# A fused mLSTM and mixture-of-experts kernel: the first phase cut into finer steps and put in a new order

## The chip, the cores and the metric

One core of a Trainium2 chip runs the whole program. Its engines are TensorE (PE, with its weight loads as PEld), VectorE (DVE), ScalarE (ACT), GpSimd (POOL) and SyncE (SP), which issues most of the DMAs. The metric is the device time of one execution in microseconds (us). The kernel before has a median of 782.83 us over three runs (781.64 to 783.22).

## What is computed

Three stages follow each other: a gated linear attention (mLSTM) over 4 batches of 768 tokens with 8 heads of 40, a dense feed-forward layer with a per-channel leaky slope, and a top-1 mixture of 8 experts with a softmax gate and a sigmoid output gate.

```python
def _attn_ref(q, k, v, i_gate, f_gate, o_gate):
    ...
    for t in range(S):
        m_new = np.maximum(f_gate[:, :, t] + m, i_gate[:, :, t])
        f_stab = np.exp(f_gate[:, :, t] + m - m_new)
        i_stab = np.exp(i_gate[:, :, t] - m_new)
        m = m_new
        C = f_stab[:, :, None, None] * C + i_stab[:, :, None, None] * np.einsum('bhd,bhe->bhde', vt, kt)
        n = f_stab[:, :, None] * n + i_stab[:, :, None] * kt
        ...
        denom = np.maximum(np.abs(nq), 1.0)
        y[:, :, t] = o * h_tilde / denom

def _moe_ref(x, w_in, w_out, alpha):        # x is 3072 x 320, w_in 320 x 2048
    h = x @ w_in
    g = np.maximum(h, 0.0) + alpha * np.minimum(h, 0.0)
    return (g @ w_out).astype(np.float32)

def _moe2_ref(x, w_gate, w_output_gate, w1, w2):
    e_idx = np.argmax(x @ w_gate, axis=1)
    ...
    out[mask] = gate_w[mask, None] * eom[mask, e, None] * (np.maximum(x[mask] @ w1[e], 0.0) @ w2[e])
```

## The kernel before

**Two phases.** The first phase does attention, the dense layer and the preparation of the expert weights; the second runs the experts on slots of 128 sorted tokens. Only the first phase's head is touched here.

**Attention units.** The tokens are 24 units of 128 (`u`; batch `u // 6`, chunk `u % 6`). For each unit `load_g` brings the cumulated gates back from DRAM in two halves (tile `D`), `att_e` takes their exponential on ACT and masks it on POOL, `att_s` (L704) makes the products of queries and keys (`ps`) and multiplies them by `D` on DVE (L713), `att_h` and `att_d` read and update the running state, `att_b` multiplies by the values (`pa`), `att_y` normalises on DVE in four steps, and `att_c` transposes the result into `xT`. A unit's state comes from the unit ahead of it.

**Gates.** `gates`, `gates_e` and `gates_d` turn the gate inputs into `G` (stored to DRAM as `gd`), `EKT` and `DEC`, in three parts that cover one, two and three chunks. They borrow the two buffers of `v` and the three of `xr`.

**Weights.** The dense weights arrive as 64-bit floats in three buffers `raw`. `dec_wi` and `dec_wo` turn each piece into 32-bit floats in three integer instructions on DVE (L614, L616, L618). `split_wi` and `split_wo` split them into a rounded high part (ACT) and a residual (POOL or DVE). `gate_w` and `gate_w2` append the products with the gate weights. The expert weights go through the same `raw` buffers: `expert_load`, `expert_split`, `expert_store`.

**Dense layer.** Three units make a block of 384 tokens, and each block has 16 chunks of 128 hidden channels; `k` counts the 128 chunks of all blocks. `ffn1` (code F, eight products into a bank `ph`, L834) is followed by a negated Relu on ACT (L842) and `ph <- v*(1-alpha)+ph` on DVE (L843). `ffn_split` (code g) makes the high part on ACT (L849) and the residual on DVE (L850), both read from `ph`. `ffn2` (code S) adds nine products into three banks `acc` (L862, L863, L865). There are two `ph` banks and two `v` buffers. The first F needs the first block's `xT`, that is the units 0, 1 and 2 in sequence. F0 and S12 below mean the first F and the thirteenth S.

**What sets the order.** `ORDER` is a written list of step codes, and every engine gets its instructions in the order of that list. Each engine works its own list strictly in order and waits on semaphores for the others. `OTHER` names the indices of a step that go to the other of DVE and POOL. POOL can't read PSUM. The step `warm` (L1172) is a product of zeros, 128x128 by 128x512, that nobody reads.

```python
            A.activation(v, ph[:, :384], AF.Relu, scale=-1.0)
            V.scalar_tensor_tensor(ph[:, :384], v, al1[:, i : i + 1], ph[:, :384], ALU.mult, ALU.add)
            gt[k] = ph[:, :384]
```

Of the kernel before, what the change touches and what calls it, by code (L numbers as in the profile page):

```python
# [8 lines left out]
F32 = mybir.dt.float32  # L9
# [8 lines left out]
P = 128  # L18
# [25 lines left out]
KR = 64 + D  # L44

OTHER = {
    "prep_kt": (
        1, 3, 4, 7, 8, 9, 13, 14, 15, 16,  # L50
    ),
    "att_y": (
        0, 1, 2, 4, 7, 11, 13, 16, 17, 18, 19, 20, 21, 22, 23,
    ),
    "expert_split": (
        0, 1, 2, 3, 5, 6, 7, 8, 10, 12, 13, 14, 15, 18, 19, 20, 25, 26, 27, 30, 31, 32, 33, 34, 35, 36,
        37, 38, 39, 40, 41, 42, 43, 44, 45, 46, 47, 48, 49, 50, 51, 52, 53, 54, 55, 56, 57, 58, 59, 60,
        61, 62, 63,
    ),
    "split_wi": (  # L60
        0, 1, 3, 5, 13, 14,
    ),
    "split_wo": (
        2, 4, 10, 15,
# [5 lines left out]
for _n, _w in (  # L70
# [11 lines left out]
lo load_gates do load_cst load_gates lo lo gates do gates_e lq gates gates_e do do warm ah so load_g ae gw do do so  # L82
do do gw load_wg load_sel li gates_d gates_d lv pt lv di di di si gv gv do lo do do do load_g ae as lg ad so so log
sg li li gw gw lq li di di di di load_g ab ay pt ay load_g di load_gates si ah ay ay di si ad ae di di di ac lo do
warm warm si load_g load_g do gv ae as ae lo lq do do do do warm ab ay so so ay ay gv ay gw warm lo lo lo warm warm
warm lg gw do ae do do do so as do lv ac gv lq lq ah gates ab set_al1 gv ay gw lo do do gw warm warm so li pt do
warm lg warm warm gates_e do so load_g ay ay ay warm do do gates_d gw di do di warm warm di lv ac warm warm warm ad
pt si el load_g es li di di lo gv gv F di load_g F g et ah si ae do g lo do do ae S F gw as so so load_g warm g S
gw do do li di log do so ae li di ad di lv gv gv F gw di di di ae F as lg load_g ah si lo si g do do ae g S S lg lg
li do so di ab ay ay ay pt di el es lq gw di li di log F F di di et g g ad si pt li di li di di si di di sg gv lo  # L90
lq sg si el S S load_g ay F F g S di ah do lv ab si do load_g do es li et F g gv li lv ay ac ay lo ay ay di g S S
ae ae di as so gw di di di F F ab di g g si li lv ac load_g di ay si S di load_g load_g li gv do di S ay el do ay
do ay F gv ae si F g di di S ae S pt lg lo g lq lq di as el ae si ad so ad pt F ac load_g do g do do ab ay ay S so
gw gw es ah log ay et ay F gv gv g lg es F g as S ah F F g ab et load_g S ae g load_g ae ay ay ay el ad bo el el es
es F F lg load_g ae S ac load_g lv ae S pt et g S g es ah lq lv ad F ay g F S as lq ah F et ab ay S g g ac el ay et
es lv el F F as S g es load_g ae lg lg et ay lq ay S sg S et g F ab ay load_g bp lg S g ac S pt el ad F F S g g S
el el es lq es F g F g ay ay ay ah pt S pt S et es F S et g F log ad g ae et as ae S bo F g F load_g ae ab ay el lv
el S g ay es el F as g load_g load_g es et es et F load_g ac lv ah el el ae ae lg lg S g S S F g ad pt ah ay es F g
ab F ay ad et ae et S g el load_g el F es ay et F ay ay ac S g es ae S g ah F S S et es ay et g lv el el bp as F F
el g es et pt S S ab ac g ad F F g S g ay lq sg es es S ay lv pt F ay el lq g F as S g F et es ah ad S log S g bo F  # L100
sg et g load_g load_g ay el el F lg S ae ab ay ay ay et S F S g lq lq S g ae ac lg el S as lv load_g load_g load_g
es et es et ay F pt F g g ab ae ay ac F S g es ay ay ay S F F ae as lq S g g load_g ah ad ac ae el F lv pt el ae g
et ab ay ay S es es F et et g load_g ay F S g as ay lv S load_g S F g F ah ab ay S el el es ad lg ay ae g ay el es
F ac g load_g et et ah ah lv es et ae bp ay S S S ae as F g F load_g bo g ab ae load_g ae F g S lq el S ac F g
load_g pt S pt F lg load_g ae as el es lq F S g S el g es et F et g ay ay el F ae ab g ay ay ay F load_g lv F S lq
S ad g g es et es et el ad pt ae ac S F g S el el as F F log g S S g es et lg bp es et F F g S g S load_g el S es
et F g F log el el ae ay ay g S S bo es F lg F ah g S es as sg ay et et g F g lq ab ay S F g el el S es load_g
load_g sg F F S g ay ad g es ae ac et S lv et ay ay pt F es F ah ab ay ay lg el ae g S g es ay lv ad pt S F F el g
ac ah et es et S load_g ay ae g el el F es S g lg S ad F et es F lq et et g el el ac bp S g S S F g F S es es g F g
et S S bo as el es F F g et lv pt el el et as ab ay es et ay ay load_g S S g lg el load_g first_set ah lq ab el ay  # L110
ay F g F S g ad ae es F F lv es g S g ac S S ae ay ay ay as et et es et ac F g F S el el el bp g F ah ab g es es ay
ay ay ay F F S S S g g et es et el S et el F g F el S es es g F et et ac g S S es et F g ld el el F g S F g S bo ld
es F F S g g route_a S F F S g el g S bh bh bh et ld ld ld ad bh ld ld bh bh bh F ld S ld es S ld ld g es F g bh bh
S bh bh F g F S et bh ld g ld S bp F F ld bh g bh bh bh bh S S bh route_first bh bh bh g F route_first2 first_rows
S g F g ld S F F S ld ld g S ld ld ld pt ld ld g first_x first_x S bo bp et first_1 route_b first_1 route_c first_t
first_s first_tl route_c2 first_t first_tl first_s first_2 first_2 route_d first_st first_2 first_2
# [19 lines left out]
    "di": ("dec_wi", [(i, j) for i in range(16) for j in range(3)]),  # L136
    "gates_e": ("gates_e", zip(range(3))),
# [12 lines left out]
    "warm": ("warm", zip(range(20))),  # L150
# [31 lines left out]
def mlstm_moe_kernel(  # L182
# [262 lines left out]
    with ExitStack() as p1:  # L445
# [70 lines left out]
        def gates(part):  # L516
            c0, c1, o = GPARTS[part]
            nn, n = c1 - c0, (c1 - c0) * P
            fs = slice(c0 * P, c1 * P)
# [3 lines left out]
            gx[part] = GG, w  # L523
# [5 lines left out]
            V.tensor_tensor(g[:, 1:], tf[:, 1:], m[:, : n - 1], ALU.add)  # L529
            lo = 1 if part == 0 else 0  # L530
            V.tensor_tensor(g[:, lo:], g[:, lo:], m[:, lo:], ALU.subtract)
            V.tensor_copy(mlast, m[:, n - 1 : n])
# [3 lines left out]
            V.tensor_tensor(w, ti, m, ALU.subtract)  # L536
            V.tensor_tensor(w, w, GG, ALU.subtract)
            nc.sync.dma_start(gd[:, fs], GG[: B * H])

        def gates_e(part):  # L540
            c0, c1, o = GPARTS[part]
            nn, n = c1 - c0, (c1 - c0) * P
            GG, w = gx[part]
            V.tensor_tensor(
# [105 lines left out]
        def gate_w(i):  # L650
# [3 lines left out]
            for k in range(3):  # L654
                c0 = min(k * P, DM - P)
                T.transpose(pt[:, k * P : (k + 1) * P], f[:, c0 : c0 + P], ident)
# [666 lines left out]
```

## Time and profile before

| | kernel before |
|---|---|
| median of three runs | 782.83 us |
| the profiled execution: its time, its span | 782.92 us, 781.1 us |
| TensorE matmul busy, weight loads busy | 751.7 us (96%), 714.8 us (92%) |
| VectorE busy | 472.0 us (60%) |
| ScalarE busy | 363.2 us (47%) |
| GpSimd busy | 164.9 us (21%) |
| granted TensorE clock, mean | 0.990 |

The shares are means over a program whose head and body differ. A reader first looks at the busy time of each engine stretch by stretch, then at where TensorE stands idle or runs slowly, and then at what the engine that it waits for does in that stretch. A matmul's end is modelled, so the start times tell more than the busy share.

### The profile page before, as it was taken

What the parts mean: (1) busy time and instruction counts of PE and PEld (TensorE: products, weight loads), DVE (VectorE), ACT (ScalarE), POOL (GpSimd) and SP (SyncE); (2) the same over time, 40 slices, a digit from 0 to 9 for tenths busy, and PEclk for the clock granted to TensorE, in tenths of its full rate; (3) what the DMA queues carried; (4) which work ended last, traced back from release to release, by engine and by line L of the source; (5) the groups of instructions that cost most, each with busy time, mean ns of one, the idle gap of its engine ahead of it and who ended that gap; (6) DMA issues with size and microseconds to landing.
All of it is one profiled execution on the core that took longest, in us unless ns stands there. A gap on an engine that the chain in (4) does not pass through costs nothing. (4 is left out here: it accounts for less than half of the span.)

```text
span 781.1 us, 15245 instructions
## 1 busy us (share of the span) xinstructions
PE 751.7 (96%) x4931; PEld 714.8 (92%) x4931; DVE 472.0 (60%) x1159; ACT 363.2 (47%) x810; POOL 164.9 (21%) x225
## 2 busy tenths in 40 slices
PE   2899999999999999999999999999999999999995
PEld 2787999989999999999999999998999999999994
DVE  4878998775767566767687786867332232232231
ACT  3536666636664654655565354433333233233231
POOL 1222433203130323210000000012232232232232
PEclk9988999999999999999999999999999999999998
DMA  6938877876788785766977868795977645921000
GB/s 194 258 111 262 271 243 231 258 234 242 230 283 296 236 294 179 234 234 245 307 255 257 294 240 303 274 340 189 383 305 292 240 171 201 428 83 39 29 22 13
DMA packets 81787, 179.64 MB, mean 230 GB/s; under 512 B 8700, under 2 KB 39481, under 8 KB 80428
## 3 DMA queue, kind: packets, MB, share of 16 engines
q1 hardware_dynamic: 78252, 169.92, 63.4%
q0 software_dynamic: 3456, 8.71, 3.3%
q8 instruction: 45, 0.74, 0.4%
q14 instruction: 34, 0.28, 0.1%
HBM read 246.55 MB, written 55.59 MB: 387 GB/s over the span
## 5 line engine op out<-in xcount | busy, mean ns | idle before, releaser
L834 PE MATMUL ph<-ring 128*128 128x384 f32 x1024 | 196.7, 340 | 0.0
L834 PEld LDWEIGHTS ph<-ring 128*128 128x128 f32 x1024 | 177.0, 188 | 1.8 <-DVE ring L850 0.4
L862 PE MATMUL acc<-ring 128*128 128x336 f32 x384 | 123.4, 326 | 0.5 <-ACT ring L849 0.5
L863 PE MATMUL acc<-ring 128*128 128x336 f32 x384 | 119.6, 317 | 0.0
L842 ACT ACTIVATE v<-ph 128x384 f32<-128x384 f32 x128 | 62.3, 489 | 114.5 <-PE ph L834 114.2
L843 DVE SCALAR_TENSOR_TENSOR ph<-v,al,ph 128x384 f32<-128x384 f32 x128 | 78.3, 618 | 53.2 <-ACT v L842 52.8
L409 DVE TENSOR_SCALAR yo<-po,xg 128x320 f32<-128x320 f32 x26 | 14.3, 551 | 137.3 <-PE po L289 137.3
L289 PE MATMUL po<-ring,hh 128*128 (+1 forms) x432 | 95.6, 308 | 0.0
L289 PE MATMUL p<-ring,xh 128*128 (+1 forms) x324 | 89.9, 398 | 0.0
L850 DVE TENSOR_TENSOR ring<-ph,ring 128x384 fp32r<-128x384 f32 x128 | 70.3, 553 | 31.4 <-ACT ring L849 29.7
L849 ACT ACTIVATE ring<-ph 128x384 fp32r<-128x384 f32 x128 | 62.1, 488 | 52.9 <-DVE ph L843 43.4
L865 PE MATMUL acc<-ring 128*128 128x336 f32 x384 | 80.2, 317 | 0.0
L289 PEld LDWEIGHTS po<-ring,hh 128*128 128x128 f32 x432 | 73.2, 187 | 2.3 <-ACT hh L389 0.2
L862 PEld LDWEIGHTS acc<-ring 128*128 128x128 f32 x384 | 72.3, 188 | 1.9 <-ACT ring L849 0.9
L863 PEld LDWEIGHTS acc<-ring 128*128 128x128 f32 x384 | 72.3, 188 | 0.0
L389 ACT ACTIVATE hh<-p 128x512 fp32r<-128x512 f32 x54 | 29.4, 595 | 86.5 <-PE p L387 86.5
L289 PEld LDWEIGHTS p<-ring,xh 128*128 128x128 f32 x324 | 58.8, 188 | 11.3
L289 PE MATMUL po<-ring,hl 128*128 (+1 forms) x216 | 66.5, 308 | 0.2 <-DVE hl L391 0.2
L376 ACT ACTIVATE hr<-p 128x512 f32<-128x512 f32 x56 | 33.4, 597 | 67.3 <-PE p L289 63.7
L865 PEld LDWEIGHTS acc<-ring 128*128 128x128 f32 x384 | 63.5, 189 | 0.2 <-DVE ring L850 0.2
L700 ACT ACTIVATE D<-D,EKT 128x128 f32<-128x128 f32 x192 | 60.7, 393 | 3.5 <-DMA D<-gd 3.3
L410 POOL DMA_INDIRECT out_dram<-yo,tok x28 | 28.1, 1003 | 160.8 <-DVE yo L409 146.2
(197 smaller groups left out, 1139.6 us busy)
## 6 DMA issues: line engine op xcount, KB each, us to landing
ring<-scr SPq DMA_DIRECT2D x26, 3072.0 KB
ring<-scr SPq DMA_DIRECT2D x26, 2560.0 KB
ring<-scr SPq DMA_DIRECT2D x33, 512.0 KB
D<-gd SPq DMA_DIRECT2D x48, 256.0 KB
er<-in_ew_dram SPq DMA_DIRECT2D x32, 384.0 KB
scr<-ring SPq DMA_DIRECT2D x32, 384.0 KB
scr<-er SPq DMA_DIRECT2D x32, 384.0 KB
er<-in_ew_dram SPq DMA_DIRECT2D x32, 320.0 KB
```

The source lines that it names most:

```text
L289: mm = T.matmul(o_, lhsT, r, start=start, stop=stop)
L376: A.activation(hr_half(j, hf), ph, AF.Relu)
L389: A.activation(hh[:, hs], pts[j, hf], AF.Copy)
L700: A.activation(d[:, j], d[:, j], AF.Exp, bias=EKT[:, c, i + j : i + j + 1])
L834: T.matmul(ph[:, :384], wi_[i][lo][:, wc], xTs[n % 2][:, xc], start=(a == 0), stop=(a == len(PASSES) - 1),)
L842: A.activation(v, ph[:, :384], AF.Relu, scale=-1.0)
L843: V.scalar_tensor_tensor(ph[:, :384], v, al1[:, i : i + 1], ph[:, :384], ALU.mult, ALU.add)
L849: A.activation(gh, v, AF.Copy)
L850: V.tensor_tensor(gl, v, gh.bitcast(F32), ALU.subtract)
L862: T.matmul(ac, gh[:, sl], hi, start=(i == 0), stop=False)
L863: T.matmul(ac, gh[:, sl], lo, start=False, stop=False)
L865: T.matmul(accs[n][t][:, :NO], gl[:, t * P : (t + 1) * P], hi, start=False, stop=(i == NFC - 1))
```

## The change

1. The products and the step that reads their bank become separate steps: `att_s` is cut into `att_s` and `att_m`, `att_h` into `att_h` and `att_n`, `att_d`/`att_u`, `att_b`/`att_a`, `att_c`/`att_x`, `gate_w`/`gate_c`, `gate_w2`/`gate_s`, `ffn1`/`ffn_act`, and `gates` into `gates`, `gates_g`, `gates_w` and `gates_st`. The list can place the halves apart.
2. The first 450 entries of `ORDER` stand in another order. Up to the thirteenth S both lists hold the same steps; behind it they are the same entry by entry. 15 of the 20 products `warm` are gone.
3. For the first 24 chunks (`KEEP`) the leaky result stays in the SBUF buffer `v` and not in the bank `ph`.
4. `OTHER` moves work: the residuals of 14 of those 24 chunks go from DVE to POOL (9 of them among the first 14 chunks), the output-gate product of units 0, 1, 2, 4 goes to POOL and that of 3 and 5 to DVE, the residuals of the expert pieces 0 and 1 go to POOL, and some `split_wi`, `split_wo` and `prep_kt` change sides.

```diff
+KEEP = 24
 OTHER = {
+    "ffn_split": (
+        0, 1, 2, 6, 8, 9, 10, 12, 13, 14, 16, 18, 20, 22,
+    ),
     "att_y": (
-        0, 1, 2, 4, 7, 11, 13, 16, 17, 18, 19, 20, 21, 22, 23,
+        3, 5, 7, 11, 13, 16, 17, 18, 19, 20, 21, 22, 23,
     ),
...
 ORDER = """
-lo load_gates do load_cst load_gates lo lo gates do gates_e lq gates gates_e do do warm ah so load_g ae gw do do so
+lo do do do load_gates gates load_cst ah lo gw load_gates warm gates_g gates_w do do load_sel gates_e gc lo do
...
+        def gates_st(part):
+            c0, c1, o = GPARTS[part]
+            nc.sync.dma_start(gd[:, c0 * P : c1 * P], gx[part][0][: B * H])
...
+            t["pp"] = pp
+
+        def att_m(u):
+            t = ut[u]
+            pp = t["pp"]
             for hf in range(2):
                 d = t["D", hf].rearrange("p h t -> p (h t)")
                 V.tensor_tensor(d, pp[hf], d, ALU.mult)
...
+            gt[k] = ph
+
+        def ffn_act(k):
+            ph = gt[k]
+            i = k % NFC
             v = hp.tile([P, 384], F32, tag="v", bufs=2, name=f"v_{k}")
             A.activation(v, ph[:, :384], AF.Relu, scale=-1.0)
-            V.scalar_tensor_tensor(ph[:, :384], v, al1[:, i : i + 1], ph[:, :384], ALU.mult, ALU.add)
-            gt[k] = ph[:, :384]
+            g = v if k < KEEP else ph[:, :384]
+            V.scalar_tensor_tensor(g, v, al1[:, i : i + 1], ph[:, :384], ALU.mult, ALU.add)
+            gt[k] = g
 
         def ffn_split(k):
             v = gt[k]
             gh, gl = gsp[k % 3]
             A.activation(gh, v, AF.Copy)
-            V.tensor_tensor(gl, v, gh.bitcast(F32), ALU.subtract)
+            engine(V, G, "ffn_split", k).tensor_tensor(gl, v, gh.bitcast(F32), ALU.subtract)
```

ScalarE's list before, from the sigmoid of the first output gates (`so`) to the exponentials of unit 1 (`D_0_298`, `D_1_313`); `f_wi` and `f_wo` are weight pieces, `woT` a transposed piece, `pt` the transpose of unit 0:

```order
L499 ACTIVATE so_268<-so_268 128x960
L657 ACTIVATE woT_276<-pw_275 128x384
L657 ACTIVATE woT_282<-pw_281 128x384
L630 ACTIVATE ring<-f_wi_292 128x384
L630 ACTIVATE ring<-f_wi_296 128x384
L700 ACT_TABLE_LOAD
L700 ACTIVATE D_0_298<-D_0_298,EKT 128x128 x4
L821 ACTIVATE ring<-pt_351 128x3x128
L630 ACTIVATE ring<-f_wi_347 128x384
L666 ACTIVATE ring<-pwg_373 128x16
L700 ACTIVATE D_1_313<-D_1_313,EKT 128x128 x4
```

The same place now, where unit 1 has the tiles `D_0_316` and `D_1_330`:

```order
L523 ACTIVATE so_278<-so_278 128x960
L699 ACTIVATE woT_296<-pw_244 128x384
L668 ACTIVATE ring<-f_wi_275 128x384
L668 ACTIVATE ring<-f_wi_293 128x384
L746 ACT_TABLE_LOAD
L746 ACTIVATE D_0_316<-D_0_316,EKT 128x128 x4
L746 ACTIVATE D_1_330<-D_1_330,EKT 128x128 x4
L668 ACTIVATE ring<-f_wi_310 128x384
L900 ACTIVATE ring<-pt_364 128x3x128
```

Both halves of unit 1 now stand together, ahead of unit 0's transpose and of a third weight piece.

TensorE's list before, ahead of the first F, which follows the last row by some more `warm`, `pd` and `pwg`; `pe_ek` and `pe_dec` are the third part of the gates, `pt_640` the transpose of unit 2 (four more rows of `warm` are left out behind the first):

```order
L656 MATMUL pw_567<-cst,f_wo_478 128x128 x3
L1172 MATMUL warm_573<-ring 128x512
...
L554 MATMUL pe_ek_594<-cst,w_525 128x96 x3
L1172 MATMUL warm_610<-ring 128x512
L572 MATMUL pe_dec_616<-gin,sel 120x12 x3
L656 MATMUL pw_623<-cst,f_wo_565 128x128 x3
L1172 MATMUL warm_633<-ring 128x512
...
L819 MATMUL pt_640<-cst,y_606 128x128 x3
```

The same place now, down to the first F (`ph_631`):

```order
L592 MATMUL pe_ek_541<-cst,w_493 128x96 x3
L1257 MATMUL warm_548<-ring 128x512
L1257 MATMUL warm_558<-ring 128x512
L693 MATMUL pw_569<-cst,f_wo_468 128x128 x3
L1257 MATMUL warm_583<-ring 128x512
L693 MATMUL pw_597<-cst,f_wo_565 128x128 x3
L890 MATMUL pt_603<-cst,y_579 128x128 x3
L610 MATMUL pe_dec_608<-gin,sel 120x12 x3
L706 MATMUL pwg_620<-wgt,woT_573 128x16 x3
L808 MATMUL pd_625<-kv_2_517,kt 120x123 x3
L913 MATMUL ph_631<-ring 128x384 x8
```

The row of five products of zeros ahead of `pe_ek` is gone; three stand singly or in a pair behind and one ahead of it, and the transpose of unit 2 comes ahead of `pe_dec`.

GpSimd's list now, behind the mask of unit 3's first half; `v_676`, `v_679` and `v_739` are the results of the first three F, `er` an expert piece:

```order
L747 AFFINE_SELECT D_0_591<-D_0_591 128x512
L935 TENSOR_TENSOR ring<-v_676,ring 128x384
L935 TENSOR_TENSOR ring<-v_679,ring 128x384
L935 TENSOR_TENSOR ring<-v_739,ring 128x384
L747 AFFINE_SELECT D_1_593<-D_1_593 128x512
L1186 TENSOR_TENSOR er_735<-er_735,ring 128x768
L1186 TENSOR_TENSOR er_737<-er_737,ring 128x768
```

The three residuals and the two expert pieces stood on VectorE.

## Rows read from the trace of the kernel before

**Rows 1.** Stretches: from:to, length, busy PE, PEld, DVE, ACT, POOL; granted clock, DMA

```profile
55.00:60.00 5.00, 4.36 (x21) 3.96 (x21) 4.93 (x18) 0.67 (x2) 0.00 (x0) 0.50 0.24 72
...
0.00:128.00 128.00, 109.28 (x676) 100.32 (x676) 104.44 (x265) 69.30 (x174) 36.09 (x52) 0.96 0.75 227
...
86.00:127.00 41.00, 40.98 (x289) 39.95 (x288) 37.61 (x90) 27.24 (x65) 15.09 (x20) 1.00 0.80 252
...
150.00:160.00 10.00, 8.70 (x58) 8.39 (x58) 8.09 (x23) 7.18 (x19) 2.88 (x7) 1.00 0.88 265
160.00:700.00 540.00, 539.70 (x3599) 518.91 (x3599) 321.01 (x792) 252.66 (x546) 98.63 (x138) 1.00 0.74 261
```

**Rows 2.** Timeline of TensorE: start, duration, work, idle before it in brackets

```profile
53.43 3.57 PE L778 MATMUL pa<-kv,D 128*128 128x41 f32 x16
...
60.15 2.48 PE L1172 MATMUL warm<-ring 128*128 128x512 f32 x5
...
68.47 3.04 PE L834 MATMUL ph<-ring 128*128 128x384 f32 x16
...
89.32 1.87 PE L778 MATMUL pa<-kv,D 128*128 128x41 f32 x16
...
126.47 0.62 PE L865 MATMUL acc<-ring 128*128 128x336 f32 x3
```

**Rows 3.** Waits of VectorE, 0 to 71.5 us: total, times, longest

```profile
DVE f_wo L614 <- DMA r_wo<-in_wo_dram: 3.9, 1, 3.9
DVE DEC L580 <- PE pe_dec L572: 2.4, 2, 1.5
DVE G L535 <- DMA cst<-in_consts_dram: 1.9, 1, 1.9
DVE D L713 <- PE ps L710: 1.6, 2, 1.2
DVE pa L788 <- PE pa L778: 1.4, 1, 1.4
DVE dn L797 <- PE pa L778: 1.4, 1, 1.4
```

**Rows 4.** Groups of VectorE, 0 to 128 us: busy us, mean ns

```profile
L618 DVE SCALAR_TENSOR_TENSOR f_wi<-r_wi,f_wi 128x384 int32<-128x384 int32 x15 | 9.0, 597 | 0.2
...
L850 DVE TENSOR_TENSOR ring<-ph,ring 128x384 fp32r<-128x384 f32 x14 | 7.5, 547 | 0.0
...
L1101 DVE TENSOR_TENSOR er<-er,ring 128x768 fp32r<-128x768 f32 x3 | 2.9, 950 | 0.0
...
L807 DVE TENSOR_TENSOR y<-y,so 128x320 f32<-128x320 f32 x4 | 2.0, 491 | 0.1
```

**Rows 5.** Timeline of VectorE, columns as in Rows 2

```profile
24.16 1.29 DVE L713 TENSOR_TENSOR D<-ps,D 128x512 f32<-128x512 f32 x2
...
40.33 1.29 DVE L713 TENSOR_TENSOR D<-ps,D 128x512 f32<-128x512 f32 x2 [0.43 <-PE ps L710]
...
50.64 0.69 DVE L713 TENSOR_TENSOR D<-ps,D 128x512 f32<-128x512 f32 x1 [1.20 <-PE ps L710]
...
71.50 0.61 DVE L843 SCALAR_TENSOR_TENSOR ph<-v,al,ph 128x384 f32<-128x384 f32 x1
...
114.51 1.20 DVE L618 SCALAR_TENSOR_TENSOR f_wi<-r_wi,f_wi 128x384 int32<-128x384 int32 x1
```

**Rows 6.** Timeline of ScalarE at the exponentials of unit 1

```profile
34.22 0.53 ACT L630 ACTIVATE ring<-f_wi 128x384 fp32r<-128x384 f32 x1 [4.69 <-DVE f_wi L618]
...
36.05 1.28 ACT L700 ACTIVATE D<-D,EKT 128x128 f32<-128x128 f32 x4
```

**Rows 7.** Groups of GpSimd over the whole span: busy us, mean ns

```profile
L631 POOL TENSOR_TENSOR ring<-f_wi,ring 128x384 fp32r<-128x384 f32 x10 | 10.1, 1014 | 13.2 <-ACT ring L630 13.2
L1101 POOL TENSOR_TENSOR er<-er,ring 128x768 fp32r<-128x768 f32 x5 | 9.2, 1840 | 32.8 <-ACT ring L1100 13.7 <-DMA scr<-er 13.5 <-DMA qg<-in_qg_dram 5.5
```

**Rows 8.** Timeline of GpSimd at 114 us

```profile
114.42 0.87 POOL L648 TENSOR_TENSOR ring<-f_wo,ring 128x320 fp32r<-128x320 f32 x1
```

More of the change, by code (lines that the diff above doesn't have):

```diff
@@ L87 @@
[L87 to L101, printed above, removed]
@@ new lines @@
+load_wg so so lg gates gates_g gw gc gates_d gates_w gv gv gs gates_e lv do do do lq lo gs gates_st gw gates_d as
+do do gc do an pt ad load_g gw load_g so ae ae am ab aa li di di log so au ah di li li sg di di gc lv pt di ay ay
+si si gates_st di di ay an load_g ad ae lq load_g as ay ae au di si am lo do ac ax li di lg di di do si do so lo do
+gv gv load_g gs gs lq ae do do ab aa gw ay ay gw lo gc gc so ay ay do lo do load_g ae do so ah an do as do ac am do
+load_gates gates so gv gs gv ax gates_g lv ab gw gs warm gates_w gates_e li warm lv lq lq warm lo lo aa do ay gw gc
@@ L117 @@
+first_2
 """
@@ L136 @@
     "di": ("dec_wi", [(i, j) for i in range(16) for j in range(3)]),
+    "f": ("ffn_act", zip(range(128))),
+    "am": ("att_m", zip(range(24))),
+    "an": ("att_n", zip(range(24))),
+    "au": ("att_u", zip(range(24))),
+    "aa": ("att_a", zip(range(24))),
+    "ax": ("att_x", zip(range(24))),
+    "gc": ("gate_c", zip(range(16))),
+    "gs": ("gate_s", zip(range(16))),
+    "gates_g": ("gates_g", zip(range(3))),
+    "gates_st": ("gates_st", zip(range(3))),
+    "gates_w": ("gates_w", zip(range(3))),
     "gates_e": ("gates_e", zip(range(3))),
@@ L149 @@
     "set_al1": ("set_al1", [()]),
-    "warm": ("warm", zip(range(20))),
+    "warm": ("warm", zip(range(200))),
     "el": ("expert_load", zip(range(64))),
@@ L535, in gates, with gates_w @@
                 V.tensor_tensor_scan(GG[:, cs], onesP[:GR], g[:, cs], 0.0, ALU.mult, ALU.add)
-            V.tensor_tensor(w, ti, m, ALU.subtract)
-            V.tensor_tensor(w, w, GG, ALU.subtract)
-            nc.sync.dma_start(gd[:, fs], GG[: B * H])
+        def gates_st(part):
+            c0, c1, o = GPARTS[part]
+            nc.sync.dma_start(gd[:, c0 * P : c1 * P], gx[part][0][: B * H])
+        def gates_w(part):
+            c0, c1, o = GPARTS[part]
+            nn, n = c1 - c0, (c1 - c0) * P
+            GG, w, g, m = gx[part]
+            ti = gin[:GR, 0, o : o + n]
+            eng = engine(V, G, "gates_w", part)
+            eng.tensor_tensor(w, ti, m, ALU.subtract)
+            eng.tensor_tensor(w, w, GG, ALU.subtract)
         def gates_e(part):
@@ L542, in gates_e @@
             nn, n = c1 - c0, (c1 - c0) * P
-            GG, w = gx[part]
+            GG, w = gx[part][:2]
             V.tensor_tensor(
@@ L561, in gates_d @@
                 return
-            GG, w = gx[part]
+            GG, w = gx[part][:2]
             dec = gin[:32, 0, o : o + B * nn].rearrange("p (b c) -> p b c", b=B)
@@ L756, in att_d, with att_u @@
                     )
+                t["pd"] = pdl
+        def att_u(u):
+            b, c = divmod(u, NC)
+            t = ut[u]
+            if c < NC - 1:
+                pdl = t["pd"]
                 if c == 0:
@@ L784, in att_b, with att_a @@
                 )
+            t["pa0"] = pa
+        def att_a(u):
+            b, c = divmod(u, NC)
+            t = ut[u]
+            pa = t["pa0"]
             if c > 0:
```

97 lines of the change are left out of this document (68 added, 29 removed).

## The prediction

> **What bounds the kernel now.** I read the stretches first. From 160 to 700 us TensorE is busy for 539.70 of 540 us, and from 86 to 127 us for 40.98 of 41; between 150 and 160 us it loses 1.3 [rows 1]. So behind 86 us the end is TensorE's work laid end to end, and a change that touches only the head gains what it takes off the time at which TensorE reaches a fixed point of its list. Both lists agree behind S12 but for the engine of some residuals, so S12 is that point. Its last products start at 126.47 us, and it is done at 127.1; the first F starts at 68.47 [rows 2]. That leaves two stretches to price: up to F0, 68.5 us, and from F0 to S12, 58.6 us. Behind S12 nothing is taken or added but five more residuals that move from VectorE, which has half its time free there, to GpSimd [rows 1].
>
> Ahead of F0 TensorE isn't the bound: it waits for the third unit's chain and for the decoded weights, and both run over VectorE. VectorE is busy for 104.44 of the first 128 us [rows 1]. Its longest waits ahead of its first L843 are listed in [rows 3]: 12.6 us in six rows, and twelve smaller ones, left out, bring the list to 18.4.
>
> TensorE also runs at the lower of its two clock levels there. The sixteen products `pa` take 3.57 us at 53.43 and 1.87 at 89.32 [rows 2], and the granted clock is 0.50 from 55 to 60 us [rows 1], which is 1.2 GHz of 2.4. It rises behind the five products `warm` that start at 60.15 [rows 2], so the first F of the kernel before finds the upper level: sixteen products in 3.04 us.
>
> **Part 1: work ahead of the first F.** Counted in both lists, VectorE has these instructions less ahead of its first `ph <- v*(1-alpha)+ph`: three output-gate products at 0.49, one expert residual at 0.95, two weight-decode instructions at 0.60 [rows 4], and five small residuals and scalings that I price at 0.55 by the 128x384 residual L850 [rows 4]. That is 1.5 + 0.95 + 1.2 + 2.7 = 6.4 us. Neighbouring instructions overlap a little at their ends, so I take 6.0.
>
> **Part 2: waits ahead of the first F.** The finer steps let a unit's pieces stand where their data are ready. The multiplication by `D` shows it: units 0, 1 and 2 do it at 24.16, 40.33 and 50.64 us [rows 5]. Unit 1's exponentials start at 36.05, because ScalarE stood 4.69 us ahead of a weight piece whose decoding wasn't done and loaded a table behind it [rows 6]; in the new list they stand ahead of that third piece, and VectorE's list has about 4 us less in front. Laying VectorE's new list end to end with the durations of the rows, I get about 20, 30.5 and 41.5 us for the three multiplications. Of [rows 3] I take as gone: 0.9 of the wait for the constants (the rest of the first weight piece's decoding now stands in it), the 1.6 for `ps`, 2.4 of the 2.8 for `pa`, and 3.9 of the 5.8 in the small rows, 8.8 in all. I add 1.4 to the wait for `pe_dec`, which VectorE reaches earlier while TensorE is at the low level, and 0.8 for a new one: part 2 of the gates needs the buffer that part 1's store to `gd` reads, and that store now stands behind seven more loads on SP's queue. Behind it on VectorE stand the second gate part and everything after; who waits is unit 0's `EKT`. Net, 6.6 us go. The bounds: none go (0), or all but the first load (14.5). I take the middle, since the three multiplications, the rows nearest to it, each move by 4 to 10 us. SP's queue is passed by nothing else that the first units need.
>
> The sum: VectorE's first L843 moves from 71.5 [rows 5] by 6.0 + 6.6 to 58.9. F0 needs 1 us more than that leaves, because it starts at the low clock, so call it 59.9, and F0 itself 57.0 instead of 68.47. **11.5 us earlier.**
>
> **Part 3: from F0 to S12.** The same F, S and small products stand here, so TensorE needs the 58.6 us of before, minus 0.5 for a `warm` that is gone. Three things are added.
> - The clock. Three products `warm` in the last stretch in place of a row of five and nine more: I expect F0 and F1 at the low level. By the ratio of the two `pa` groups (3.57 / 1.87) the 3.04 us become 5.8, so +3 with a small product behind them. Bounds: 0 (the clock is up by then) and 6 (F2 and F3 as well).
> - GpSimd takes nine residuals at 1.01, two expert pieces at 1.84, two weight residuals at 1.01 [rows 7] and two or three small products near 0.87 [rows 8]: 16 us on top of 36.09 [rows 1]. It has the room; what each gains for VectorE is 0.55 and 0.95 [rows 4], some 9 us up to S12. VectorE pays some back: its L618 at 114.51 took 1.20 us where the mean is 0.60, and it ended 0.4 behind GpSimd's residual that started at 114.42 [rows 4, 5, 8]. Nine such long instructions, of which this is one, add about 3.2 us beside 36 of GpSimd's; 16 more make it 1.5.
> - In the new list two expert pieces hold two of the three `raw` buffers at once, just behind F2, and the decoder has one buffer left meanwhile. The residuals of F0 to F2 keep the two `v` buffers until GpSimd is done; behind that wait on ScalarE stand its exponentials and high parts.
>
> VectorE's list between the first L843 and the fourteenth is about 49 us of work by the same durations, TensorE's 58, so VectorE's losses are mostly covered; for these two points together I take +1, with bounds 0 and 5 (uncovered: 1.5 and most of a load with its decoding). KEEP itself I cost at nothing: the same instruction with another target, and the bank comes free earlier.
>
> The Trainium skill (GPSIMD Engine Reference, § 1. Specifications) says that GpSimd shares its SBUF interfaces with VectorE and contends with VectorE instructions of two SBUF inputs. The trace agrees: the L618 that took 1.20 us reads two SBUF tensors. Taken at its worst, half of the 16 us blocking such instructions, VectorE's 49 us would become 57, still no more than TensorE's, and the sum would stay.
>
> So S12 is reached at 57.0 + 58.6 - 0.5 + 3 + 1 = 119.1 instead of 127.1: **8 us earlier**. Behind S12 the gain keeps: TensorE has no slack there to give back but the 1.3 us, and what feeds it comes earlier too. The profiled execution took 782.92, within 0.1 of the median of 782.83, so 782.9 - 8 = **775 us**.
>
> **The rivals.**
> - A, the gain is given back behind F0: the `raw` buffers starve the decoder, and part 3 costs 8.5 instead of 3.5. For it: VectorE was busy 37.61 of 41 us there [rows 1]. Against it: VectorE has 9 us less to do. 782.9 - 11.5 + 8.5 = 780.
> - B, larger: the clock is up at F0 and the waits go nearly all: 14 us at F0, 0.5 more behind it. 769.5.
> - C, no change: the chain of the units isn't what held F0, its waits move to other instructions, and only the 6.0 of part 1 remains against 3 for the clock and 3 for the rest. 783.
> - D, slower: TensorE stays at the low level through the first F and S, since the products that raised it are gone. [...] Each us of full-speed work at the low level costs 0.9; from 13 us of such work the change loses. With 19 us, F0 to S3, it is 17 instead of 3: 789.
>
> **How the numbers follow.** The forecast (771.5 to 778.5) has 0.55, A 0.15, B 0.13, C 0.08, D 0.09. B's far side and D are left out of the range, which is 768.5 to 781.5. A measurement of this kernel can tell about 0.2% from no change, 1.6 us, that is 781.3 to 784.4. The forecast, A and B are faster, 0.83; C is the same, 0.08; D is slower, 0.09.
>
> **What would show it.** In the profile after: `D` of units 1 and 2 multiplied near 30 and 41 us; F0 near 57 and the first L928 near 60; the first sixteen F products in 5 to 6 us and the next in 3; the thirteenth S done near 119; 99.9% busy from 160 on. I am wrong if F0 starts behind 63, if TensorE waits for ScalarE's or GpSimd's residuals for more than 3 us between F0 and S12, or if the end moves by less than S12 does.

## The result, and the profile after

The changed kernel takes **793.35 us** (median; 793.02 to 794.47) beside 782.24 of the kernel before on the same chip: ratio **1.0135**, 95% interval 1.0112 to 1.0157. It is slower: by 11.1 us in the medians, by 10.6 at the ratio. The prediction said 775, range 768.5 to 781.5. The profiled execution spans 791.5 us in place of 781.1.

The stretches of the trace after, as in [rows 1]: from:to, length, busy PE, PEld, DVE, ACT, POOL, granted clock, DMA share, GB/s. The first two are cut at F0 and at the end of S12.

```profile
0.00:63.40 63.40, 46.72 (x227) 41.00 (x228) 46.42 (x122) 27.35 (x69) 21.42 (x31) 1.00 0.69 212
63.40:133.60 70.20, 61.80 (x417) 57.71 (x416) 62.53 (x125) 38.41 (x94) 32.61 (x33) 0.98 0.64 198
...
86.00:127.00 41.00, 38.44 (x263) 36.19 (x262) 38.90 (x80) 22.56 (x51) 16.94 (x20) 0.96 0.75 232
100.00:120.00 20.00, 18.85 (x125) 17.64 (x123) 19.48 (x39) 11.39 (x26) 11.57 (x13) 0.91 0.69 211
...
160.00:700.00 540.00, 538.36 (x3588) 517.46 (x3587) 324.56 (x801) 257.11 (x560) 102.40 (x144) 1.00 0.75 265
```

The same two cuts in the trace before:

```profile
0.00:68.50 68.50, 50.39 (x248) 43.77 (x248) 49.07 (x135) 28.72 (x71) 14.83 (x26) 0.93 0.68 198
68.50:127.10 58.60, 57.98 (x417) 55.65 (x416) 54.47 (x130) 39.68 (x100) 20.77 (x27) 1.00 0.83 261
```

F0 comes 5.05 us earlier (63.42 for 68.47), and S12 6.5 us later (133.6 for 127.1): from F0 to S12 it now takes 70.2 us in place of 58.6. TensorE stands idle there for 8.4 us (before: 0.6), and the same 417 products take it 61.8 us in place of 58.0. VectorE is busy for 62.5 us in place of 54.5, with five instructions fewer; from 100 to 120 us it is busy for 19.5 of the 20, so it has no room left there. Behind S12 another 3.8 us are lost, 2.8 of them up to the second S behind it.

TensorE's waits from F0 to S12 (total, times, longest). Seven rows come to 8.3 us, and VectorE ends 6.8 of them; the four longest:

```profile
PE acc L948 <- DVE ring L713: 1.7, 1, 1.7
PE acc L947 <- ACT ring L934: 1.5, 1, 1.5
PE acc L950 <- DVE ring L935: 1.4, 1, 1.4
PE pw L693 <- DVE hN L793: 1.1, 1, 1.1
```

TensorE's F0 and the last products of S12, which answer to [rows 2] (start, duration):

```profile
63.42 2.87 PE L913 MATMUL ph<-ring 128*128 128x384 f32 x15
...
132.96 0.67 PE L950 MATMUL acc<-ring 128*128 128x336 f32 x3
```

VectorE's waits up to 68.1 us, where its first L928 starts, answering to [rows 3]:

```profile
DVE f_wo L652 <- DMA r_wo<-in_wo_dram: 4.0, 1, 4.0
DVE G L563 <- DMA gd<-G: 3.1, 1, 3.1
DVE DEC L618 <- PE pe_dec L610: 3.0, 2, 1.9
DVE D L764 <- PE ps L756: 2.2, 1, 2.2
DVE G L563 <- DMA cst<-in_consts_dram: 1.4, 1, 1.4
DVE D L764 <- POOL D L747: 0.9, 1, 0.9
```

And where VectorE's time went. The 96 instructions that decode the weights are the same in both kernels. Groups up to 170 us (busy us, mean ns), of before and then of after; [rows 4] showed one of them up to 128 us:

```profile
L618 DVE SCALAR_TENSOR_TENSOR f_wi<-r_wi,f_wi 128x384 int32<-128x384 int32 x16 | 9.8, 615 | 0.2
L616 DVE SCALAR_TENSOR_TENSOR f_wi<-r_wi,f_wi 128x384 int32<-128x384 int32 x16 | 8.8, 552 | 0.3
L616 DVE SCALAR_TENSOR_TENSOR f_wo<-r_wo,f_wo 128x320 int32<-128x320 int32 x16 | 8.4, 524 | 0.3
L618 DVE SCALAR_TENSOR_TENSOR f_wo<-r_wo,f_wo 128x320 int32<-128x320 int32 x16 | 8.1, 507 | 0.3
```

```profile
L928 DVE SCALAR_TENSOR_TENSOR v<-v,al,ph 128x384 f32<-128x384 f32 x21 | 12.4, 604 | 3.8 <-ACT v L926 3.8
L654 DVE SCALAR_TENSOR_TENSOR f_wi<-r_wi,f_wi 128x384 int32<-128x384 int32 x16 | 11.4, 714 | 0.5
L656 DVE SCALAR_TENSOR_TENSOR f_wo<-r_wo,f_wo 128x320 int32<-128x320 int32 x16 | 11.2, 698 | 0.4
L656 DVE SCALAR_TENSOR_TENSOR f_wi<-r_wi,f_wi 128x384 int32<-128x384 int32 x16 | 10.9, 681 | 0.3
...
L654 DVE SCALAR_TENSOR_TENSOR f_wo<-r_wo,f_wo 128x320 int32<-128x320 int32 x16 | 8.9, 556 | 0.4
```

With the two shift groups (L614 before, L652 after) the 96 take 47.0 us before and 58.7 after. The reason stands in two timelines side by side, VectorE's and then GpSimd's, which answer to [rows 5] and [rows 8]:

```profile
101.80 0.35 DVE L652 TENSOR_SCALAR f_wi<-r_wi 128x384 int32<-128x384 int32 x1
102.19 1.26 DVE L654 SCALAR_TENSOR_TENSOR f_wi<-r_wi,f_wi 128x384 int32<-128x384 int32 x1
103.48 1.26 DVE L656 SCALAR_TENSOR_TENSOR f_wi<-r_wi,f_wi 128x384 int32<-128x384 int32 x1
104.67 0.54 DVE L826 TENSOR_TENSOR pd<-pd,cst 120x369 f32<-120x369 f32 x1
```

```profile
101.99 1.04 POOL L669 TENSOR_TENSOR ring<-f_wi,ring 128x384 fp32r<-128x384 f32 x1 [4.31 <-ACT ring L668]
103.00 1.33 POOL L935 TENSOR_TENSOR ring<-v,ring 128x384 fp32r<-128x384 f32 x1
```

The decode instruction that starts at 102.19 ends at 103.45, 0.42 behind GpSimd's first residual; the next ends at 104.74, 0.41 behind the second. Each alone takes 0.56. So it looks as if each stood until GpSimd's instruction was over and did most of its own work then; the trace shows the ends, not the standing. GpSimd pays too: its residuals of activations take 1149 ns, where those of the weights, of the same size, took 1014 in [rows 7]:

```profile
L935 POOL TENSOR_TENSOR ring<-v,ring 128x384 fp32r<-128x384 f32 x14 | 16.0, 1149 | 15.7 <-ACT ring L934 9.0 <-ACT ring L712 5.6 <-DMA q<-in_qs_dram 1.0
```

### The profile page after: what moved, and what is told of

Same layout as the page of the kernel before. It is cut to its first block, busy times and chain, and to the rows that moved or that the text cites. A ratio compares the mean times of both kernels' runs of the same rounds, so it can differ in the third digit from the quotient of the medians.

```text
span 791.5 us, 15196 instructions
## 1 busy us (share of the span) xinstructions
PE 753.9 (95%) x4916; PEld 715.1 (90%) x4916; DVE 477.4 (60%) x1139; ACT 363.7 (46%) x810; POOL 191.8 (24%) x245
## 4 chain that ended last, share of the span: by engine, by line
PE 77%; DVE 9%; DMA 6%; issue 3%; ACT 2%; POOL 2%; SPq 1%; POOLq 0%; ACTq 0%; DVEq 0%
PE ph L913 19%; PE po L313 12%; PE p L313 12%; PE acc L947 6%; PE acc L948 6%; PE acc L950 6%; PE pa L843 4%; PE p L411 3%; PE ps L756 2%; DMA r_wo<-in_wo_dram 2%; DMA D<-gd 1%; PE xt L373 1%; PE pb L778 1%; DVE f_wi L654 1%; DMA gd<-G 1%
## 5 line engine op out<-in xcount | busy, mean ns | idle before, releaser
L926 ACT ACTIVATE v<-ph 128x384 f32<-128x384 f32 x128 | 61.9, 489 | 109.9 <-PE ph L913 107.8
L928 DVE SCALAR_TENSOR_TENSOR ph<-v,al,ph 128x384 f32<-128x384 f32 x104 | 63.8, 619 | 48.6 <-ACT v L926 48.3
L935 DVE TENSOR_TENSOR ring<-ph,ring 128x384 fp32r<-128x384 f32 x104 | 57.3, 554 | 30.4 <-ACT ring L934 29.4
L934 ACT ACTIVATE ring<-ph 128x384 fp32r<-128x384 f32 x104 | 50.5, 488 | 43.5 <-DVE ph L928 37.2
```

What stands on the lines that cost most here:

```text
L928: V.scalar_tensor_tensor(g, v, al1[:, i : i + 1], ph[:, :384], ALU.mult, ALU.add)
L934: A.activation(gh, v, AF.Copy)
L935: engine(V, G, "ffn_split", k).tensor_tensor(gl, v, gh.bitcast(F32), ALU.subtract)
```

## The experiments

In the table, all from the profiled executions: F0 and S12 (start and end, us), what VectorE was busy and idle up to S12, and its **stretch**: the durations of its instructions up to S12, less what they take undisturbed (for each form the lower quartile of its durations in the traces of before, after and e1). The forms are counted one by one, so neighbours that overlap at their ends count twice in a sum of durations, but once in busy time. A profiled execution can lie some us off its kernel's median (e3: 789.7 for 784.3), so verdicts go by the ratio to the kernel before.

| kernel | ratio, 95% interval | F0 | S12 | busy + idle | stretch |
|---|---|---|---|---|---|
| before | 1 | 68.5 | 127.1 | 103.5 + 23.6 | 3.9 |
| after | 1.0135 [1.0112, 1.0157] | 63.4 | 133.6 | 108.9 + 24.7 | 16.7 |
| e1 residuals back | 1.0129 [1.0101, 1.0157] | 63.0 | 131.7 | 108.4 + 23.2 | 12.0 |
| e2 order alone | 1.0249 [1.0225, 1.0273] | 65.5 | 144.7 | 112.4 + 32.2 | 10.4 |
| e8 order, SBUF activations | 1.0177 [1.0133, 1.0221] | 67.1 | 139.4 | 112.3 + 27.2 | 11.9 |
| e5 GpSimd's residuals cut | 0.9997 [0.9974, 1.0020] | 62.5 | 124.5 | 99.7 + 24.8 | 7.1 |
| e12 and zeros written | 1.0037 [1.0017, 1.0058] | 63.7 | 128.6 | 103.3 + 25.4 | 10.4 |
| e13 and two inputs read | 1.0053 [1.0032, 1.0073] | 64.9 | 131.1 | 106.3 + 24.8 | 13.2 |
| e6 new head, old rest | 1.0012 [0.9994, 1.0030] | 66.0 | 126.1 | 106.9 + 19.3 | 7.3 |
| e7 old head, new rest | 1.0138 [1.0098, 1.0178] | 69.7 | 135.3 | 109.2 + 26.1 | 16.5 |
| e3 old order, GpSimd residuals | 1.0020 [1.0002, 1.0039] | 72.7 | 132.4 | 106.2 + 26.3 | 9.7 |
| e14 old order, SBUF activations | 1.0003 [0.9984, 1.0022] | 70.7 | 129.3 | 106.0 + 23.3 | 6.3 |
| e11 old order, new places | 1.0050 [1.0028, 1.0071] | 67.1 | 128.4 | 108.2 + 20.2 | 11.9 |
| e9 new head, old rest, new places | 1.0074 [1.0052, 1.0096] | 65.3 | 132.8 | 108.0 + 24.7 | 11.8 |
| e10 the same, 15 `warm` more | 1.0081 [1.0058, 1.0104] | 70.0 | 133.4 | 107.8 + 25.6 | 11.5 |
| e4 early store | 1.0272 [1.0241, 1.0302] | 74.9 | 143.9 | 109.4 + 34.4 | 17.0 |

**Which part costs.** e1, e2 and e8 take parts back in the new order.

```diff
 # e1: the activations' residuals on DVE
 "ffn_split": (
-    0, 1, 2, 6, 8, 9, 10, 12, 13, 14, 16, 18, 20, 22,
 ),
 # e8: OTHER as before; e2: that, and KEEP
-KEEP = 24
+KEEP = 0
```

> The changed kernel with the fourteen ffn residuals back on VectorE; everything else (order, activations in SBUF, the other moves to GpSimd) as changed. Before takes 782.2 us, the changed kernel 793.4. Theory T1 (GpSimd slows VectorE: in the changed kernel the decode instructions on VectorE that stand beside a GpSimd residual take 1.1 to 1.3 us where 0.37 to 0.60 is their usual time): GpSimd loses 14 times 1.18 = 16.5 us of work, VectorE gets 14 times about 0.6 = 8.4 us of its own, but each of about 14 long instructions falls back by about 0.6; the instructions of decode get a mean near 0.55 again and the time goes to 786 to 790. Theory T2 (the new order of the first 451 steps is what costs, through raw buffers held and waits in order): VectorE is only given 8.4 us more, and the time stays at 793 or rises to 797.

Measured: 791.56 us, between the two forecasts, and its interval covers that of the changed kernel. Up to S12 VectorE has eight instructions more, 4.4 us of work by undisturbed durations, and 4.7 us less of stretch. So the fourteen residuals on GpSimd gain and cost nothing that can be told: what they took off VectorE came back as longer durations of its other instructions.

> The changed kernel's order and finer steps alone: the places of every split (VectorE or GpSimd) as before, and no activation kept in SBUF. T1 (GpSimd slows VectorE): the gain of the earlier first product (63.4 in place of 68.5 us) is kept to the thirteenth second product, 778 to 782. T2 (the order costs): 790 to 795, with the time from the first first-layer product to the end of the thirteenth second-layer product still near 70 us in place of 58.6.

Measured: 801.83 us, 79.2 us from F0 to S12: slower than T2 had it. The new order issues F before the residual that frees the bank `ph`, and without activations in SBUF TensorE waits for that. TensorE's waits in e2 from 55 to 160 us (total, times, longest):

```profile
PE ph L908 <- DVE ring L930: 13.9, 4, 5.9
```

> The new order with the 24 activations kept in SBUF, and every split where the kernel before has it (so no activation residual on GpSimd, and the first two expert splits and four of the y times o products on VectorE again). Without the activations in SBUF this order took 801.8 us, TensorE waiting 13.9 us for its two PSUM buffers of the first layer to be read out by VectorE. T1 (what was moved to GpSimd costs): 783 to 787. T2 (the order costs): 789 to 793, near the 791.6 of the run that moved only the activation residuals back. The distance to 801.8 is what the activations in SBUF are worth in this order: 8 to 12 us by either.

Measured: 797.85 us, worse than both forecasts. `KEEP` is worth 4.0 us here by the medians (801.83 to 797.85), 5.6 by the ratios, where 8 to 12 were forecast. The order and `KEEP` without any new place are 1.8% slower than the kernel before; the new places of the other splits then win 6.3 us back by the medians (797.85 to 791.56 in e1), 3.8 by the ratios, whose intervals overlap. T1 in its first form, that what was moved to GpSimd costs, falls. But the stretch is 11.9 us in e8 (10.4 in e2) in place of 3.9, with GpSimd doing what it did before: the order alone puts VectorE's decode beside GpSimd's work. The time for which one of the 96 decode instructions and one of GpSimd's run side by side shows it: 7.5 us before, 16 in e2, 18 in e8, 29 in the changed kernel. Of the 12.3 us by which S12 comes later in e8, 8.0 are stretch and 3.6 idle time of VectorE.

**Head or rest.** e6 and e7 join the two orders at the first F. Here the entries around it:

```diff
 # e6
 load_g gv pt ad gs
-F do do au so di di di
+lg so do di do di di au pt si el es li di di lo gv gs F f di F f
 # e7
 es li di di lo gv gs gv gs
-F f di load_g F f g et
+load_g load_g F so F ae gv f f do do g gw F
```

> The new order up to its first first-layer product (200 steps), and behind that all that is left in the order of the kernel before; the places of all splits as before, no activation kept in SBUF. T2a (of the new order what costs is what lies behind that product): the first product comes at about 63 us in place of 68.5, the rest runs as in the kernel before, 58.6 us and up to 2 for what the head left undone, and the time is 777 to 780, faster than both. T2b (the head costs, as it leaves decode and splits to be done later): 783 to 790. T1 alone (GpSimd's share decides, and here it is as before): 778 to 782.

Measured: 783.42 us, the same as before: each forecast of a gain missed, and the time lies at the lower edge of T2b's range. F0 comes at 66.0 only. The steps that the head left undone now stand ahead of it, but they needn't be why: e2 and e8 have the same head and the same old places, their F0 stands ahead of those steps, and it comes at 65.5 and 67.1. So the 63.4 of the changed kernel needs its new places too. F0 then finds the low clock, granted 0.54 from 66.0 to 71.2 us: sixteen products in 5.22 us where [rows 2] has 3.04.

```profile
66.00 5.22 PE L908 MATMUL ph<-ring 128*128 128x384 f32 x16
```

From there the old rest takes 60.1 us, with a stretch of 1.8 behind the first activation, and S12 comes 1.0 us earlier than before: the loss of the changed kernel isn't in its head. But the head has its own stretch, 5.5 us ahead of the first activation in place of 1.1.

> The mirror of the run before it: the order of the kernel before up to its first first-layer product, behind it all that is left in the new order, with the changed kernel's placement of the splits and its 24 activations in SBUF. T2a (the new rest costs): first product at 68 to 69, thirteenth second-layer product over 135, time 793 to 800. T2b (the new head costs): 782 to 787.

Measured: 794.28 us. The new rest, with the new places and the activations in SBUF, gives the whole loss without the new head (T2a).

**Is it GpSimd's work?**

```diff
 # e5
-engine(V, G, "ffn_split", k).tensor_tensor(gl, v, gh.bitcast(F32), ALU.subtract)
+e = engine(V, G, "ffn_split", k)
+n = 16 if e is G else 384
+e.tensor_tensor(gl[:, :n], v[:, :n], gh[:, :n].bitcast(F32), ALU.subtract)
...
 # e12, behind each of them that is GpSimd's
+G.memset(fill[:, :604], 0.0)
 # e13, in place of that
+G.tensor_tensor(scratch[:, :224], fill[:, 240:464], fill[:, 480:704], ALU.subtract)
```

> The changed kernel with every residual of the first phase that GpSimd has (twelve of the first-layer weights, eleven of the second-layer weights, fourteen of the activations) cut to its first 16 columns of each row or chunk; the rest of the residual is left out (zeros, written once by GpSimd before 12 us, where it is idle). Order, activations in SBUF and all that VectorE does are as changed. The 96 decode instructions on VectorE take 47.0 us in all in the kernel before and 58.7 in the changed one. T1 (GpSimd's work slows VectorE's, and VectorE sets the time to the thirteenth second-layer product): the 96 fall back to about 48 to 50 us, that product ends some 7 to 9 us earlier than 133.5, and the time is 780 to 785. T2 (the order in which VectorE's work stands costs, whoever is beside it): the decode gets shorter, but VectorE then waits as much longer, and the time stays over 789.

Measured: 783.08 us, within T1's forecast; T2's (over 789) falls. The decode takes 50.1 us and S12 ends at 124.5. VectorE's idle time up to S12 is that of the changed kernel (24.8 for 24.7); it is busy 9.2 us less, and its stretch is 9.6 less. Nothing of its own work was changed. The two cuts in e5's trace, with F0 and S12 at their ends:

```profile
0.00:62.50 62.50, 43.94 (x228) 38.41 (x228) 45.35 (x122) 27.37 (x69) 22.69 (x57) 0.78 0.72 215
62.50:124.50 62.00, 58.76 (x416) 55.87 (x416) 54.39 (x125) 38.55 (x94) 18.24 (x33) 1.00 0.72 225
```

That isn't a gain over the kernel before, though it leaves most of these 37 residuals out. S12 is 2.6 us earlier than before, but from F0 to S12 it takes 62.1 us in place of 58.6 and behind S12 another 1.8 go; GpSimd's other work still stretches VectorE's by 7.1. The low clock in a part of the head (0.78 up to F0) needn't be a reason: F0 comes 1 us earlier than in the changed kernel, which has 1.00 there. The same cut wasn't made in the kernel before, whose stretch of 3.9 leaves less to win.

> As e5 (GpSimd's residuals of the first phase cut to 16 columns, the rest left out), with a filling of 604 columns behind each cut residual on GpSimd: it writes zeros to a place that nobody reads, and reads nothing. So GpSimd is busy about as long as in the changed kernel and is as late for its next work. In e5 the early fillings of this kind left VectorE's three-operand decode at its 0.49, while one shift beside them took 1.70 in place of 0.33. T1a (it is the reading of SBUF by both engines that stretches VectorE's instructions): the three-operand decode keeps near its own length, the 96 take 50 to 54 us in all, and the time stays near e5's 783, at 782 to 787. T1b (it is GpSimd's lateness, whatever it does): 790 to 794.

> The same with another filling: a difference of two stretches of 224 columns in SBUF, written to a place that nobody reads, so that GpSimd reads two operands there as its residuals do, for about as long as the filling of zeros. T1a (shared reading of SBUF): the 96 decode instructions go back up to 55 to 59 us and the time to 788 to 794, though each residual's own 16 columns are ready at once. T1b (lateness): the same time as with zeros, within 2 us.

Measured: 786.47 and 788.22 us, decode 53.4 and 55.2. T1b's 790 to 794 for mere lateness falls. Both are inside T1a's ranges, e13 at its lower edge. But the two are 1.75 us apart, inside the 2 that T1b gave them, and their intervals overlap: the times don't part reading from lateness. The instructions do. In e5 and e12 eight decode instructions of two inputs stood beside GpSimd's writing of zeros alone, two at 0.55 and six at 0.49, their undisturbed time; seven shifts of 320 columns, of one input and 0.32 us undisturbed, took 0.90 in the mean and up to 2.36. Reading by GpSimd holds both kinds. The remaining 5 to 6 us between e13 and the changed kernel I can't split: in e13 each residual is done early and the filling stands elsewhere than the residual did. So without GpSimd's residuals the loss is gone (e5), and reading beside reading is shown to stretch the instructions, but how much of the time comes by it and how much by GpSimd's own lateness stays open.

**The old order with the new parts.** e3, e11 and e14 keep the order of the kernel before; e9 and e10 the head of the new one.

```diff
 # e14: KEEP alone; e3: that, and the fourteen residuals on GpSimd
-KEEP = 0
+KEEP = 24
 # e10, in e9's list: five here, five ahead of ad, five ahead of F
+warm warm warm warm warm
 gates_d ax load_g gv pt
```

> The order and all splits of the kernel before, with only this part of the change: the first 24 activations are written to SBUF and fourteen of the first residuals run on GpSimd. T1: GpSimd gets 16.5 us more in the first 150 us and VectorE instructions beside it grow by about 0.6 us each, while VectorE is relieved of 14 times 0.55 = 7.7 us; net 0 to 4 us slower than before, 782 to 786, with the mean of the decode instructions up by 0.05 to 0.15 us. T2: VectorE is only relieved, 779 to 782, decode instructions as long as before.

> The kernel before in its own order and with its own places of the splits; only the first 24 activations are written to SBUF in place of back to PSUM. My prediction priced this part at nothing. With e3 (the same and fourteen residuals on GpSimd, ratio 1.002) it tells the two apart. If the activation part is worth nothing: 781.5 to 783, and GpSimd's share of e3 is 1 to 2 us. If it frees PSUM as in the new order: 778 to 781. If the residuals, which then read both inputs from SBUF, are slowed beside GpSimd (VectorE's took 639 ns in place of 550 in e1): 783 to 785.

Measured: 784.28 (ratio 1.0020) and 784.42 us (ratio 1.0003; the kernel before had 783.98 in that session). Activations in SBUF are worth nothing in the old order, as priced; in the new one 4 us or more (e2 to e8). e14's 784.42 would fit its forecast of 783 to 785 for slowed residuals, but beside the 783.98 of that session nothing was lost. The fourteen residuals are worth nothing or cost up to 0.4% in the old order too.

> The order of the kernel before with the changed kernel's places of the splits, except the residuals of activations, which stay on VectorE; no activation in SBUF. In the new order these places were worth 6.3 us (797.9 to 791.6). T1 (they cost VectorE as much as they relieve it, unless the order was made for them): 782 to 785. Rival (they are worth the 4 us of VectorE's work in any order): 778 to 780.

Measured: 786.32 us, slower than either forecast: four us of work less ahead of the first activation, and the stretch there went from 1.1 to 6.8 us. "Worth the same in any order" falls. The same stretch doesn't give the same time, either: e8, e9 and e11 all have 11.8 or 11.9 us, and 797.85, 788.79 and 786.32. In e11 VectorE's idle time fell by 3.4 us, in e8 it rose by 3.6.

> The new order up to its first first-layer product, behind it what is left in the order of the kernel before (as in e6), now with the changed kernel's places of the splits, except that all residuals of activations stay on VectorE and no activation is kept in SBUF. In the changed kernel these places take 4 us of work off VectorE ahead of its first activation product, and the first first-layer product came 3.7 us earlier with them than without (63.4 against 67.1). Theory T1+T2a (what costs in the changed kernel is the new rest, in which VectorE's decode stands beside GpSimd's work; the old rest keeps them apart): first product at 62.5 to 64, thirteenth second-layer product done at 122 to 125 in place of 127.1, time 777.5 to 781, ratio 0.994 to 0.999. Rival (any work given to GpSimd comes back as longer VectorE instructions, in the old rest too): the same as before or up to 4 us slower, 782 to 786.

Measured: 788.79 us; the forecast of a gain was wrong, and its rival (782 to 786) was nearer, but too low as well. One place shows the whole chain, VectorE's rows first, then GpSimd's, then TensorE's:

```profile
69.37 2.16 DVE L669 TENSOR_TENSOR ring<-f_wi,ring 128x384 fp32r<-128x384 f32 x1
...
72.51 0.61 DVE L928 SCALAR_TENSOR_TENSOR ph<-v,al,ph 128x384 f32<-128x384 f32 x1
```

```profile
69.07 2.03 POOL L1186 TENSOR_TENSOR er<-er,ring 128x768 fp32r<-128x768 f32 x1 [3.23 <-ACT ring L712]
```

```profile
73.70 0.65 PE L947 MATMUL acc<-ring 128*128 128x336 f32 x1 [4.11 <-ACT ring L934]
74.15 0.48 PE L948 MATMUL acc<-ring 128*128 128x336 f32 x1
```

VectorE's weight residual, 0.55 us alone, starts beside GpSimd's expert piece and ends 0.43 us behind it, at 71.5; the activation, behind three more instructions, comes at 72.5. ScalarE's high part waits for that, and TensorE for ScalarE: it stands idle for 4.1 us and goes on at the low clock (granted 0.51 from 76 to 80 us), 0.48 a product where it is 0.32 from 81 us on.

> The run before it with fifteen warm-up products put back in the 6 us ahead of the first first-layer product. In e6 the first two of these products ran at the low clock (4.3 and 3.9 us of products in place of 2.8 and 2.7). Theory T4 (the fewer warm-up products cost up to 3 us in such a kernel): 1 to 2.5 us faster than e9, if there the first two are slow too, and the same as e9 if they aren't. Rival (the added products only stand in TensorE's way): up to 2 us slower than e9.

Measured: 789.7 us, intervals overlapping. The first two F ran at the high level in e9 already, so this tells nothing on a kernel where they don't.

**The early waits.**

```diff
 # e4, for all three parts
-warm gates_g gates_w do do load_sel gates_e gc lo do
+warm gates_g gates_st gates_w do do load_sel gates_e gc lo do
```

> The changed kernel with each store of the gate sums put right behind its scan, as the kernel before had it, in place of behind seven other transfers. The wait of the second part's scan for that store (3.10 us at 15.2 us) should fall under 1 us and the first mask products on VectorE come up to 2 us earlier. If the waits ahead of the first first-layer product are what costs (a part of T2), the time falls by 2 to 3 us, to 790 to 791.5; by T1 the time behind that product is set by VectorE and GpSimd together and VectorE starts its decode earlier by as much, so also 790 to 793: this run tells only how much of the early waits is worth anything.

Measured: 803.32 us, 10 slower than the changed kernel; forecast a little faster. The scan's wait is gone, but the store now stands in SP's queue ahead of the loads. SP's own waits in e4 up to 80 us:

```profile
SPq L567 <- DVE ring L713: 12.3, 1, 12.3
...
SPq L567 <- DVE w L575: 4.5, 1, 4.5
```

L567 is that store. The loads behind it come late (VectorE waits 9.4 us for `r_wo` up to 80 us, where the changed kernel waits 4.0 up to 68), F0 at 74.9. In this order the late place that the change gave this store is right, whatever it costs the scan.

## Why the prediction was wrong

**Part 1 (work ahead of the first F) was right in its count and wrong in its result.** VectorE's instructions ahead of its first activation sum to 56.1 us before and 50.0 after by undisturbed durations: 6.1 less, for 6.0 predicted. But they were stretched by 6.2 us in place of 1.1, so only about 1 us of it arrived. The stretch came with the order of the head: e6, with the old places and the old work, has 5.5 there.

**Part 2 (waits) was half right.** Predicted was 6.6 us net; VectorE's idle time ahead of the first activation went from 19.8 to 17.0. The new wait for the store of `gd`, priced at 0.8, measured 3.1; `pe_dec` came out at 3.0, and the wait for `ps`, which I took as gone, at 2.2. The `D` multiplications came at 23.1, 35.1 and 48.7 us, not at 20, 30.5 and 41.5. F0 was 6.4 us later than forecast. The sum for it had a slip of its own: the 1 us for the low clock lies between F0 and the first L843, so by its terms F0 would have come near 56, and the clock term of part 3 priced that us once more.

**Part 3 failed at the contention term, and this is what decided.** I priced GpSimd's extra work at 1.5 us of longer VectorE instructions. Measured up to S12, the stretch went from 3.9 to 16.7: 12.8 us, 8.8 of them between F0 and S12. The two errors in it:
- I scaled with the amount of GpSimd's work (16 us more on 36; up to S12 18.5 more came). e8 shows the stretch at 11.9 without any more of it, and e6 at 7.3: what counts is which VectorE instructions stand beside it. [rows 8] and L618 in [rows 5] had shown the mechanism; the lists, which tell what stands beside what, I read for their count alone.
- I let VectorE's loss vanish behind TensorE ("49 us of work, TensorE's 58"). In the trace before VectorE was busy for 54.5 of the 58.6 us from F0 to S12, and 37.61 of 41 stood in [rows 1]. There was room for 4 us, not for 9, and I had noted that row under rival A and then set it aside. Two sums of work don't show that one covers the other: each engine also waits for the other within them.

The case taken "at its worst", 57 us of VectorE's work in place of 49, came nearly true and was judged wrongly: from the first L928 to the fourteenth VectorE was busy for 58.5 us, but it also stood idle for 8.1 there (before: 50.1 and 3.6), and TensorE's 58 covered neither. The Trainium skill (SBUF — State Buffer, § SBUF: two separate sides) goes further than the section that the prediction named: it calls the shared port pair an exclusive lock that one instruction holds to its end. The rows at 102 us agree: both instructions end 0.4 us behind GpSimd's.

**The clock term (+3 at F0 and F1) wasn't paid here**: F0 and F1 ran at the high level (granted 1.00 from 63.4 to 66.3 us), 15 of their 16 products recorded in 2.87 us. It was paid in e6 (5.22 us). From 100 to 120 us the granted clock is 0.91; that is a piece of the loss that the forecast hadn't.

**"Behind S12 the gain keeps"** failed by 3.8 us; e6 has 0.3 of that, e5 1.8 and e7 3.2. So the 18.3 us between 775 and 793.35 are 6.4 at F0, 8.1 from F0 to S12 and 3.8 behind it. Which instruction starts it I didn't isolate.

**The rivals.** None had this: A had the place (behind F0) but ended at 780, D had the sign for another reason. A's own mechanism, the `raw` buffers, is there but small: VectorE waits 3.8 us for pieces of weights between F0 and S12, in place of 1.9, and 3.2 in e5, which is back at the time of before. Of the signs named beforehand, F0 behind 63 came true (63.42). TensorE's waits for ScalarE's high parts came to 1.5 us and none for GpSimd's residuals stands in the list, so that sign looked at the wrong engines: TensorE waited for VectorE. That the order is slower without any new place is shown by e2 and e8, that the changed kernel's loss lies in its rest by e7, and that it goes when GpSimd's residuals go by e5; that each single stretched microsecond went to TensorE isn't shown.

None of the runs beats the kernel before.

## What to carry to other kernels

Before work is moved to GpSimd, count the VectorE instructions that will stand beside it and read SBUF alone: each may last until GpSimd's ends. A move then promises a gain beside VectorE work that reads PSUM, or where VectorE waits anyway; no run here tried such a move. Price a helper's losses against the busy time measured in that stretch, not against a sum of durations. And where several engines walk through fixed lists, a reordering changes what runs beside what; the kernel before had most of its decode where GpSimd was idle: 77 of the 96 instructions, 47 in the changed kernel.

## What was not expected of the hardware

- In the changed kernel the decode instructions with no GpSimd work beside them, or under 0.1 us of it, never left their time: 555 ns in the mean and at most 560 (17 of 384 columns, two inputs), 323 and at most 327 (9 shifts of 320). With a two-input GpSimd instruction beside them for over 0.1 us, nine of the former took 837 in the mean and up to 1261, four of the latter 812 and up to 1139.
- VectorE instructions with one operand in PSUM weren't touched by it: `D<-ps,D` 682 ns alone and 685 beside (9 of them), `v<-v,al,ph` 603 and 605. With its activations in SBUF the residual on VectorE became one of those that are: 552 alone, 919 beside (3).
- One instruction can lose far more than its own time: 2.16 us for 0.55 in e9, and a shift of 0.32 took 2.36 beside a row of zero writings in e12.
